# Opening of a fused attention and MLP kernel: warming matmuls, low parts, U and V loads, decoder pace

## The chip, the cores and the metric

The kernel runs on one core of one Trainium2 chip. The metric is device time in microseconds; a kernel's time is the median of its runs. The core's engines each follow their own row of instructions: TensorE (PE) multiplies matrices, VectorE (DVE), ScalarE (ACT) and GpSimd (POOL) work on tiles, and SyncE (SP) issues most transfers (DMAs).

## The reference

```python
# attention with random features, for q, k, v of shape (8, 8, 576, 64)
def phi(x):
    proj = np.einsum('bhsd,md->bhsm', x, omega)          # 128 features
    h = proj - np.sum(x * x, axis=-1, keepdims=True) / 2.0
    h = h - np.max(h, axis=-1, keepdims=True)
    return np.exp(h) / np.sqrt(m)
q_p, k_p = phi(q * scale), phi(k * scale)
kv = np.einsum('bhsm,bhsd->bhmd', k_p, v)
z = np.sum(k_p, axis=2)
num = np.einsum('bhsm,bhmd->bhsd', q_p, kv)
den = np.einsum('bhsm,bhm->bhs', q_p, z)[..., None] + 1e-06
x = (num / den), heads side by side                      # (8, 576, 512)
# then a low-rank mix over the sequence and an MLP
h = x.transpose(0, 2, 1) @ U @ V                         # rank 32
u = x + h.transpose(0, 2, 1)
out = u + np.maximum(u @ w_ch1, 0.0) @ w_ch2             # 512 -> 2048 -> 512
```

U, V and the two MLP weights come as 64-bit floats; everything else is 32-bit.

## The kernel before

Products are made in a reduced format of the same width (fp32r) from a high part and a low part of each operand: the high part is a cast, the low part the difference, and three matmuls (high by high, low by high, high by low) give one product.

**The attention.** The work is cut into 16 units: a pair of batches and a pair of heads. A unit's keys, and then its queries, are loaded as raw tiles of 64-column blocks and run through nine tiles of 128 rows. A *round* `r` has nine *steps* and handles two parts side by side: at first the keys of units 0 and 1, then in each round the keys of one unit and the queries of an earlier one. The second round (steps 9 to 17) takes keys 2 and queries 0, the third (steps 18 to 26) keys 3 and queries 1, and so on through 144 steps. The tile names are by place and not by content: `kt` is the first part's raw tile, `qt` the second's, so that `qt<-in_k_dram` is the keys of unit 1.

For three steps at a time a part is turned (`turn`, L614, a transpose on DVE into `xT`), cast (`high`, L618, on ACT into `xh`) and its low part is made (`low`, L622, on POOL into `xl`). `xT` has two buffers. A step then consists of `project` (L741 to L743, six matmuls into `p_p`, of which two buffers exist), `peak` (L749, the row maximum, on DVE into `nm`), `exp` (L756, four exponentials on ACT into `e`, three buffers), `use` (for keys a product with the values, L653 into `p_kv`; for queries two transposes, L679 into `p_q`, and a copy L684), and for queries `combine` (L692, L699, into `p_n`) and the normalizing of L709 to L724. A table `DELAY` sets how many steps after its own number each of these is written. The kernel is written step by step; a scheduler then orders the instructions of each engine, except that those wrapped in `K` (`keep_in_program_order`) stay in the order written among themselves.

**The loads.** All but a few loads of the attention are issued by SP, one after another, in the order written: omega, keys 0 and 1, their values, then in steps 0 and 1 of each round the keys and queries of the next round, and the values behind them.

**The decoder.** U, V and the weights are decoded from 64-bit to 32-bit floats beside the attention by a generator, `decoding`. A call of `advance(decoder)` moves it on by one piece of a job. Its first call issues the loads of U and of the first half of V (L329 to L332, L354); after six more calls the first job starts. A job is two ACT instructions (L132, L135), three on DVE (L150, L151, L154) and one on POOL (L174); then come the casts and low parts of the result (L336 to L339 for U, L360 to L363 for V, L246 to L255 for the first MLP weight). The step loop calls `advance` at `s % 3` not 0, two steps of three, for the first 54 steps, and at every second step after that; `left` limits the calls in all.

**The warming matmuls.** At the start, before any data has come, 12 matmuls of a zero tile `idle` are written, each into a tile `p_m` of its own, of which there is one buffer (L789). They are not kept in order.

**After the attention.** The low-rank mix of a pair of batches runs beside the next rounds (`mixing`: L401, L446, L414, L422), its result goes to DRAM; then the MLP's two products run as a seven-product scheme over blocks (L979, L1357), which takes the rest of the time.

Of the kernel before, what the change touches and what calls it, by code (L numbers as in the profile page):

```python
# [29 lines left out]
def performer_mlp_kernel(ctx: ExitStack, tc, q, k, v, omega, U, V, w1, w2, out):  # L30
# [74 lines left out]
    def depth():  # L105
        return 2 * RB if roomy else RB
# [8 lines left out]

    def decoding(jobs, late, lean, base, hold=(), defer=(), wide=0):

# [11 lines left out]
        def magnitude(i):  # L129
            if i < len(jobs):  # L130
                mags[i] = jobs[i][2]()
                K(nc.scalar.activation(out=mags[i], in_=f32(raws[i][:, :, 1]), func=AF.Abs))  # L132
                if i >= lean:
                    lows[i] = dec.tile([P, PIECE], I32, name="low", tag="de", bufs=2)[:, : jobs[i][1]]
                    K(nc.scalar.activation(out=lows[i], in_=raws[i][:, :, 0], func=AF.Copy, scale=2.0**-29))  # L135

        fetch(depth())
        for _ in range(late):
# [236 lines left out]
    EARLY = 1 + 2 + 4 * EARLY_GROUPS  # L375
    left = [6 + 5 * EARLY + 3]

# [221 lines left out]
    class Part:  # L599


        def __init__(self, src, i, place):
            self.src, self.unit = src, units[i]
            self.raw = io.tile([P, 2 * S], F32, name=("kt", "qt")[place])
            self.xh, self.xl = [], []
# [14 lines left out]
        def low(self):  # L620
            self.xl.append(wk.tile([P, G * P], F32R, name="xl", bufs=4))
            nc.gpsimd.tensor_tensor(out=self.xl[-1], in0=self.turned, in1=f32(self.xh[-1]), op=ALU.subtract)  # L622

# [149 lines left out]


    units = [(pair, hp) for pair in range(NP) for hp in range(NU)]
    keys = [Keys(i, i) for i in range(2)]
# [10 lines left out]
    nc.vector.memset(idle, 0.0)  # L787
    for _ in range(12):
        nc.tensor.matmul(ps.tile([P, P], F32, name="p_m", tag="p_m"), idle, idle, start=True, stop=True)  # L789
    om = mp.tile([P, 2, D], F32, name="om", tag="y", bufs=2)  # L790
# [16 lines left out]
    pom = ps.tile([P, P], F32, name="p_q", tag="p_q", bufs=2)  # L807
    nc.tensor.transpose(pom, om.rearrange("p j d -> p (j d)"), ident)
    for j in range(2):
        r = slice(j * D, (j + 1) * D)  # L810
        nc.scalar.copy(out=omh[r, j, :], in_=pom[r])
        nc.vector.tensor_tensor(out=oml[r, j, :], in0=pom[r], in1=f32(omh[r, j, :]), op=ALU.subtract)
# [16 lines left out]
    steps = {}  # L829
    decoder = decoding([u_job(), *v_jobs(), *weight_jobs()], 6, 0, -EARLY, defer=(EARLY + 3,), wide=EARLY)  # L830
    mixers = []
    x = None
    for s in range(NR * NT + 7):
# [34 lines left out]
        for st in at("turn0"):  # L868
            for p in st.group(0):
                p.turn()  # L870
        if s % (3 if s < 6 * NT else 2):
            advance(decoder)
# [40 lines left out]
        for st in at("project"):  # L913
            st.project()
        for st in at("use0"):
            st.use(0)
# [506 lines left out]
```

## Time and profile before

| | |
|---|---|
| three runs | 1064.04, 1067.19 and 1067.72 us; median 1067.19 |
| the profiled execution | 1067.31 us, of which 1065.2 us are the span from the first to the last instruction |
| mean granted clock of TensorE | 0.99 |
| busy share of PE, DVE, ACT, POOL | 97%, 81%, 58%, 48% of the span |
| first projection (step 0), second round (step 9) | at 8.33 us and 25.00 us |
| steps 54, 90 | at about 122.8 and 196.9 us |

The profile gives for each engine when an instruction started and how long it took. In a row of the timeline stand the start and the time in us, the engine, the line of the code, the operation, the tile written and the tiles read, and in square brackets how long the engine had been idle and what released it. In a row of windows stand the stretch, its length, the busy time and number of instructions of each engine shown, the granted clock of TensorE (1.00 is full), the share of the DMA engines and GB/s. In a row of groups stand the busy time in all, the mean of one in ns, and the idle time before them. A matmul of 32-bit operands that are not fp32r is recorded twice.

### The profile page before, as it was taken

Reading aid. Unit: us, or ns where it says so; the run is one execution under the profiler, and the core shown is the slowest. Engines: PE = TensorE matmul, PEld = TensorE weight load, DVE = VectorE, ACT = ScalarE, POOL = GpSimd, SP = SyncE. Lnnn points to the kernel's source line nnn. Section 1 sums busy time; section 2 is a strip of 40 time slices with the busy share of each in tenths; the row PEclk is TensorE's granted clock in tenths of the full one; section 3 lists DMA queues with packets and bytes.
Section 4 is the critical chain, followed back from the end, with each engine's and each line's share of the span. In section 5 each row is a group of like instructions: output and inputs, shape, how many; then the busy total and the mean of one; then the engine's idle time right before and its main releaser. Section 6 shows DMA issues by size and latency. Waiting matters only on the chain. (4 is left out here: it accounts for less than half of the span.)

```text
span 1065.2 us, 23872 instructions
## 1 busy us (share of the span) xinstructions
PE 1037.9 (97%) x8497; PEld 1014.9 (95%) x8497; DVE 864.0 (81%) x1510; ACT 615.5 (58%) x1479; POOL 506.3 (48%) x453
## 2 busy tenths in 40 slices
PE   8999999999998899999999999999999999999998
PEld 7898999989987899999999999999999999999998
DVE  4798898997998876766587576779999998989995
ACT  5889889889764646445445444754344444444442
POOL 3446957777334532341234214536645445445443
PEclk9899999999999899999999999999999999999999
DMA  9788787685337665976778857965455454454451
GB/s 133 137 159 149 146 191 136 126 206 106 89 61 192 170 174 141 234 223 173 176 201 198 212 156 222 302 201 184 142 169 169 139 173 165 141 171 164 142 173 43
DMA packets 380486, 175.51 MB, mean 165 GB/s; under 512 B 275664, under 2 KB 353488, under 8 KB 375760
## 3 DMA queue, kind: packets, MB, share of 16 engines
q1 hardware_dynamic: 378000, 173.70, 62.5%
q8 instruction: 67, 1.10, 0.4%
q10 hardware_dynamic: 2368, 0.30, 0.2%
q14 instruction: 51, 0.42, 0.1%
HBM read 109.97 MB, written 63.96 MB: 163 GB/s over the span
## 5 line engine op out<-in xcount | busy, mean ns | idle before, releaser
L756 ACT ACTIVATE e<-p_p,nm 128x128 f32<-128x128 f32 x576 | 166.1, 397 | 23.5 <-DVE nm L749 16.1
L1170 POOL TENSOR_TENSOR gs<-graw 128x512 f32<-128x512 f32 x70 | 105.6, 1513 | 145.4 <-DMA graw<-g 114.3
L1196 ACT CAST gh<-gs 128x512 fp32r<-128x512 f32 x140 | 86.9, 622 | 151.5 <-DVE gs L1170 76.9
L963 ACT ACTIVATE g<-g 128x512 f32<-128x512 f32 x105 | 66.5, 634 | 171.4 <-DVE g L967 100.3
L1203 DVE TENSOR_TENSOR gl<-gs,gh 128x512 fp32r<-128x512 f32 x140 | 133.8, 963 | 17.4 <-ACT gh L1196 15.8
L622 POOL TENSOR_TENSOR xl<-xT,xh 128x384 fp32r<-128x384 f32 x96 | 97.4, 1031 | 99.4 <-ACT xh L618 85.0
L749 DVE TENSOR_REDUCE nm<-p_p 128x4 f32<-128x512 f32 x144 | 98.2, 683 | 26.1 <-PE p_p L743 9.7
L174 POOL TENSOR_TENSOR wf<-wf,low 128x512 int32<-128x512 int32 (+2 forms) x35 | 45.1, 1288 | 145.6 <-ACT g L963 111.9
L741 PE MATMUL p_p<-omh,xh 128*128 128x256 f32 x288 | 93.3, 324 | 4.5 <-ACT e L756 3.0
L1282 POOL TENSOR_TENSOR u<-u,p 128x256 f32<-128x256 f32 x72 | 75.4, 1075 | 33.0 <-DVE u L1282 30.4
L1196 ACT CAST gh<-graw 128x512 fp32r<-128x512 f32 x107 | 64.3, 621 | 39.4 <-PE p_p L1357 9.5
L1203 DVE TENSOR_TENSOR gl<-graw,gh 128x512 fp32r<-128x512 f32 x107 | 80.8, 770 | 5.9 <-ACT gh L1196 4.8
L743 PE MATMUL p_p<-omh,xl 128*128 128x256 f32 x288 | 81.6, 284 | 0.6 <-POOL xl L622 0.6
L742 PE MATMUL p_p<-oml,xh 128*128 128x256 f32 x288 | 81.4, 283 | 0.0
L1357 PE MATMUL p_p<-wh,gh 128*128 128x256 f32 x288 | 81.1, 282 | 0.0
L1357 PE MATMUL p_p<-wh,gl 128*128 128x256 f32 x288 | 81.0, 281 | 0.0
L1357 PE MATMUL p_p<-wl,gh 128*128 128x256 f32 x288 | 80.9, 281 | 0.0
L1357 PE MATMUL p_q<-wh,gh 128*128 128x256 f32 x276 | 77.7, 282 | 0.0
L1357 PE MATMUL p_q<-wh,gl 128*128 128x256 f32 x276 | 77.6, 281 | 0.0
L1357 PE MATMUL p_q<-wl,gh 128*128 128x256 f32 x276 | 77.5, 281 | 0.0
L979 PE MATMUL p_n<-uh,wh 128*128 128x256 f32 x256 | 73.2, 286 | 3.9 <-DVE g L967 3.9
L699 PE MATMUL p_n<-kv,eT 128*128 128x65 f32 x512 | 72.3, 270 | 3.0 <-ACT eT L684 1.1
(267 smaller groups left out, 4023.2 us busy)
## 6 DMA issues: line engine op xcount, KB each, us to landing
graw<-g SPq DMA_DIRECT2D x36, 1024.0 KB, 5.2
g<-g SPq DMA_DIRECT2D x282, 128.0 KB, 2.3
raw<-in_moe_w_ch_dram SPq DMA_DIRECT2D x22, 512.0 KB, 4.6
u_dram<-ut SPq DMA_DIRECT2D x36, 256.0 KB, 2.4
u<-u_dram SPq DMA_DIRECT2D x36, 256.0 KB, 2.7
out_dram<-u SPq DMA_DIRECT2D x36, 256.0 KB, 2.3
kt<-in_k_dram SPq DMA_DIRECT2D x120, 72.0 KB, 3.0
qt<-in_q_dram SPq DMA_DIRECT2D x120, 72.0 KB, 2.7
```

What stands on the lines that cost most here:

```text
L622: nc.gpsimd.tensor_tensor(out=self.xl[-1], in0=self.turned, in1=f32(self.xh[-1]), op=ALU.subtract)
L741: nc.tensor.matmul(o, part.xh[g][:, ts], oh, start=True, stop=False)
L742: nc.tensor.matmul(o, part.xh[g][:, ts], ol, start=False, stop=False)
L743: nc.tensor.matmul(o, part.xl[g][:, ts], oh, start=False, stop=True)
L749: nc.vector.tensor_reduce(out=self.nm[:, :n], in_=self.pp[:, :n], axis=AX.X, op=ALU.max, negate=True)
L756: nc.scalar.activation(out=self.e[:, j, :], in_=self.pp[:, j, :], func=AF.Exp, bias=self.nm[:, j : j + 1])
L979: K(nc.tensor.matmul(p[:, f, :], x[:, k, fs], y[:, k, :], start=first, stop=(k == 1 and y is ul), skip_group_check=True,))
L1170: K(engine.tensor_tensor(out=to, in0=self.val[x], in1=self.val[y], op=op))
L1196: K(nc.scalar.copy(out=h, in_=v))
L1203: K(nc.vector.tensor_tensor(out=l, in0=v, in1=f32(h), op=ALU.subtract))
L1282: K(engine.tensor_tensor(out=out, in0=x, in1=y, op=ALU.add))
L1357: K(nc.tensor.matmul(acc[bank][:, half, :], x[:, ks], y[:, f, :], start=(now.s == 0 and k == 0 and half == 0 and x is h and y is wh), stop ...
```

## The change

- The 12 warming matmuls become 4 ahead of the transpose of omega, 12 behind it and 6 behind the projection of step 1. Those of one group share one tile, and all are kept in order.
- The low parts of the first two groups of three steps of keys 0 and keys 1 are made on DVE, not on POOL.
- The decoder waits for six more calls before it issues the loads of U and V (`rest=6`). They are then written behind the keys and queries of the third round.
- The step loop calls `advance` two times in three steps up to step 89, not 53; `left` is larger by six. By step 90 the decoder is where it was before.

```diff
-    def decoding(jobs, late, lean, base, hold=(), defer=(), wide=0):
+    def decoding(jobs, late, lean, base, hold=(), defer=(), wide=0, rest=0):
...
+        for _ in range(rest):
+            yield
         fetch(depth())
         for _ in range(late):
             yield
...
-    left = [6 + 5 * EARLY + 3]
+    left = [6 + 6 + 5 * EARLY + 3]
...
-            self.src, self.unit = src, units[i]
+            self.src, self.unit, self.i = src, units[i], i
...
-            nc.gpsimd.tensor_tensor(out=self.xl[-1], in0=self.turned, in1=f32(self.xh[-1]), op=ALU.subtract)
+            opening = isinstance(self, Keys) and self.i < 2 and len(self.xl) < 3
+            (nc.vector if opening else nc.gpsimd).tensor_tensor(
+                out=self.xl[-1], in0=self.turned, in1=f32(self.xh[-1]), op=ALU.subtract
+            )
...
+    BUSY = 12, 6
...
-    for _ in range(12):
-        nc.tensor.matmul(ps.tile([P, P], F32, name="p_m", tag="p_m"), idle, idle, start=True, stop=True)
+
+    def busy(n):
+        none = ps.tile([P, P], F32, name="p_m", tag="p_m")
+        for _ in range(n):
+            K(nc.tensor.matmul(none, idle, idle, start=True, stop=True))
+
+    busy(4)
...
     nc.tensor.transpose(pom, om.rearrange("p j d -> p (j d)"), ident)
+    busy(BUSY[0])
...
-    decoder = decoding([u_job(), *v_jobs(), *weight_jobs()], 6, 0, -EARLY, defer=(EARLY + 3,), wide=EARLY)
+    decoder = decoding([u_job(), *v_jobs(), *weight_jobs()], 6, 0, -EARLY, defer=(EARLY + 3,), wide=EARLY, rest=6)
...
-        if s % (3 if s < 6 * NT else 2):
+        if s % (3 if s < 10 * NT else 2):
             advance(decoder)
...
             st.project()
+            if st.s == 1 and s < NT:
+                busy(BUSY[1])
```

How the rows of the engines stand: on PE, before, the warming matmuls (`p_m`) lie around the transpose of omega and between the matmuls of steps 0 and 1.

```order
L789 MATMUL p_m<-idle 128x128 x2
L808 MATMUL p_q<-ident,om 128x128
L789 MATMUL p_m<-idle 128x128 x6
L741 MATMUL p_p<-omh,xh 128x256
L742 MATMUL p_p<-oml,xh 128x256
L741 MATMUL p_p<-omh,xh 128x256
L742 MATMUL p_p<-oml,xh 128x256
L789 MATMUL p_m<-idle 128x128
L743 MATMUL p_p<-omh,xl 128x256
```

On PE now, the same place:

```order
L798 MATMUL p_m<-idle 128x128 x4
L819 MATMUL p_q<-ident,om 128x128
L798 MATMUL p_m<-idle 128x128 x12
L746 MATMUL p_p<-omh,xh 128x256
L747 MATMUL p_p<-oml,xh 128x256
L746 MATMUL p_p<-omh,xh 128x256
L747 MATMUL p_p<-oml,xh 128x256
L748 MATMUL p_p<-omh,xl 128x256
```

Three more stood between and behind the following matmuls of steps 0 and 1 before; now none stands between them, and the last six stand behind step 1's last matmul.

On DVE, before, from the first transposes of the keys (`xT`) to the first row maxima (`nm`):

```order
L614 STREAM_TRANSPOSE xT<-kt 128x384
L614 STREAM_TRANSPOSE xT<-qt 128x384
L614 STREAM_TRANSPOSE xT<-kt 128x384
L614 STREAM_TRANSPOSE xT<-qt 128x384
L749 TENSOR_REDUCE nm<-p_p 128x4 x3
```

On DVE now, up to the third row maximum:

```order
L616 STREAM_TRANSPOSE xT<-kt 128x384
L616 STREAM_TRANSPOSE xT<-qt 128x384
L625 TENSOR_TENSOR xl<-xT,xh 128x384 x2
L616 STREAM_TRANSPOSE xT<-kt 128x384
L754 TENSOR_REDUCE nm<-p_p 128x4 x2
L625 TENSOR_TENSOR xl<-xT,xh 128x384
L616 STREAM_TRANSPOSE xT<-qt 128x384
L754 TENSOR_REDUCE nm<-p_p 128x4
```

The row maxima of steps 0 and 1 now stand ahead of the fourth transpose, and the low parts stand between; the fourth of them comes behind one more transpose.

On SP's queue, before, from the queries of the second round on (`x<-in_v_dram` are the values of keys 2, `kt` and `qt` behind them belong to the third round):

```order
L594 DMA qt<-in_q_dram 32x18x32 x8
L329 DMA raw<-in_moe_U_dram 128x4x64
L330 DMA raw<-in_moe_U_dram 64x64
L331 DMA raw<-in_moe_U_dram 64x64
L332 DMA raw<-in_moe_U_dram 128x4x64
L354 DMA raw<-in_moe_V_dram 32x576 x4
L636 DMA x<-in_v_dram 128x4x64 x2
L640 DMA x<-in_v_dram 64x2x64
L636 DMA x<-in_v_dram 128x4x64 x2
L640 DMA x<-in_v_dram 64x2x64
L594 DMA kt<-in_k_dram 32x18x32 x8
L594 DMA qt<-in_q_dram 32x18x32 x8
```

On SP's queue now, the same place:

```order
L596 DMA qt<-in_q_dram 32x18x32 x8
L641 DMA x<-in_v_dram 128x4x64 x2
L645 DMA x<-in_v_dram 64x2x64
L641 DMA x<-in_v_dram 128x4x64 x2
L645 DMA x<-in_v_dram 64x2x64
L596 DMA kt<-in_k_dram 32x18x32 x8
L596 DMA qt<-in_q_dram 32x18x32 x8
L331 DMA raw<-in_moe_U_dram 128x4x64
L332 DMA raw<-in_moe_U_dram 64x64
L333 DMA raw<-in_moe_U_dram 64x64
L334 DMA raw<-in_moe_U_dram 128x4x64
L356 DMA raw<-in_moe_V_dram 32x576 x4
```

U and V have moved behind the values of keys 2 and the third round's loads; the 42 issues in front of them are the same. Further on the scheduler also orders other instructions anew on all five engines, up to about step 90 (196.9 us); from there on the rows are the same as before.

## The prediction

> **What bounds the kernel now.** I read the page first, then PE's windows of 25 us, then the first 45 us by windows cut where the clock changes and by the timelines of PE, DVE, ACT and SP. PE's row on the page and two of its windows:
>
> ```profile
> PE 1037.9 (97%) x8497; PEld 1014.9 (95%) x8497; DVE 864.0 (81%) x1510; ACT 615.5 (58%) x1479; POOL 506.3 (48%) x453
> 25.00:50.00 25.00, 22.74 (x162) 21.57 (x162) 17.72 (x44) 19.10 (x63) 10.44 (x11) 0.86 0.71 138
> 425.00:450.00 25.00, 25.00 (x213) 25.00 (x212) 17.17 (x24) 11.37 (x21) 9.22 (x7) 1.00 0.93 239
> ```
>
> PE is the bound nearly everywhere: at 425 us it starts 213 matmuls in 25 us and never stops. At 25 to 50 us it starts 162, at a granted clock of 0.86. The whole change acts before about 200 us, since both programs' rows are alike on all five engines from there on; a lead won there is carried to the end, because what follows is PE work in the same order. So the question is how much PE loses at the start and how much of it the change removes. The stretch at 25 us, first by the clock (us, PE busy, matmuls, granted clock, DMA):
>
> ```profile
> 11.11:14.53 3.42, 2.19 (x15) 1.00 0.75 165
> 24.77:28.18 3.41, 1.53 (x10) 1.00 0.75 132
> 28.18:31.59 3.41, 3.41 (x18) 0.50 0.65 154
> 31.59:35.01 3.42, 3.42 (x18) 0.50 0.67 151
> 359.30:362.70 3.40, 1.56 (x13) 1.00 0.88 274
> 362.70:366.10 3.40, 3.40 (x19) 0.50 0.71 90
> ```
>
> From 28.18 to 35.01 us TensorE had half its clock: 6.83 us, a loss of about 3.4. Ahead of it lies a window of 3.41 us in which PE was busy for 1.53; 359.30 is another such window, and the clock halved behind it too. The window at 11.11, busy for 2.19, was followed by no drop. Why PE idled at 25 us, from PE's timeline:
>
> ```profile
> 25.32 0.28 PE L743 MATMUL p_p<-omh,xl 128*128 128x256 f32 x1
> 26.90 0.39 PE L741 MATMUL p_p<-omh,xh 128*128 128x256 f32 x1 [1.30 <-ACT xh L618]
> 27.98 0.44 PE L743 MATMUL p_p<-omh,xl 128*128 128x256 f32 x1 [0.58 <-POOL xl L622]
> ```
>
> and from those of DVE and of SP's queue:
>
> ```profile
> 25.73 0.58 DVE L614 STREAM_TRANSPOSE xT<-qt 128x384 f32<-128x384 f32 x1 [2.18 <-DMA qt<-in_q_dram]
> 15.89 4.38 SPq L594 DMA_DIRECT2D kt<-in_k_dram  x8
> 20.31 5.36 SPq L594 DMA_DIRECT2D qt<-in_q_dram  x8
> 25.71 0.50 SPq L329 DMA_DIRECT2D raw<-in_moe_U_dram  x1
> 28.12 1.89 SPq L354 DMA_DIRECT2D raw<-in_moe_V_dram  x4
> 38.73 5.31 SPq L594 DMA_DIRECT2D qt<-in_q_dram  x8
> ```
>
> Step 9, the first of the second round, needs the first queries. Their eight transfers leave SP at 20.31 to 25.67, right behind the keys', and DVE has waited 2.18 us for them when it starts at 25.73. ACT's cast follows, then the matmul at 26.90, then POOL's low part, then the matmul at 27.98. This gate at 26.90 to 28.2 us is set by SP's row of issues and not by anything PE does.
>
> **The change part by part.**
>
> *The faster start (warming matmuls, low parts on DVE).* What paced steps 0 to 3, by the timelines of DVE, ACT and PE:
>
> ```profile
> 11.21 0.58 DVE L614 STREAM_TRANSPOSE xT<-qt 128x384 f32<-128x384 f32 x1 [1.16 <-DMA qt<-in_k_dram]
> 11.82 1.29 DVE L749 TENSOR_REDUCE nm<-p_p 128x4 f32<-128x512 f32 x2
> 12.54 2.18 ACT L756 ACTIVATE e<-p_p,nm 128x128 f32<-128x128 f32 x8 [0.21 <-DVE nm L749]
> 13.74 0.39 PE L741 MATMUL p_p<-omh,xh 128*128 128x256 f32 x1 [1.18 <-ACT e L756]
> ```
>
> and what a low part costs, by the page's groups:
>
> ```profile
> L622 POOL TENSOR_TENSOR xl<-xT,xh 128x384 fp32r<-128x384 f32 x96 | 97.4, 1031 | 99.4 <-ACT xh L618 85.0
> L1203 DVE TENSOR_TENSOR gl<-graw,gh 128x512 fp32r<-128x512 f32 x107 | 80.8, 770 | 5.9 <-ACT gh L1196 4.8
> ```
>
> The first two reductions stood on DVE behind a transpose that waited for its DMA until 11.21; now they stand ahead of it, and the low parts are made on DVE. DVE has no 128x384 subtraction in the trace; POOL takes 1.03 us, and DVE's of 128x512 took 0.77, three quarters of which are 0.58. I take 0.6. The first exponentials can start at about 10.9 instead of 12.54. What is late next is the fourth low part: its transfer lands at 11.21 as before, and behind it come a transpose (0.58), a cast (0.51) queued behind eight exponentials, and a subtraction. So step 4 on gains 1.2 to 1.5 us, less than the 1.6 of the exponentials. And all of that ends at the gate: SP's first 42 issues are the same in both programs, none of them waits for this work, so step 9's second half still starts at 26.90. Worth 0; only PE's idle time ahead of the gate grows, from 1.3 us to about 2.8.
>
> *Ten more warming matmuls.* Each is two records:
>
> ```profile
> 1.09 1.65 PE L789 MATMUL p_m<-idle 128*128 128x128 f32 x4 [1.09 <-DVE idle L787]
> PEld p_m L789 <- PE p_m L789: 2.4, 7, 0.4
> ```
>
> Two took 1.65 us, 0.83 each, with a pause of some 0.35 to 0.4 for the one before, which one shared tile removes: about 0.45 each. Four end before the transposed omega needs PE (3.1 us), twelve run from 3.4 to about 8.8 while clock and data are awaited anyway; the first projection stood at 8.33. The six behind step 1 fill the wait that ended at 13.74. At most 0.5 us late, in front of the gate: 0.
>
> *The clock behind the gate.* With about 2.8 + 0.6 us of idle in front of it, nearly every position of a 3.41 us window takes in 1.9 us of idle or more, as 24.77 did, so the clock drops again, at a boundary somewhere between 25.4 and 28.8, for one window or two. Two windows would end between 32.2 and 35.6, one earlier. The loss behind 28 us is then half of what is left, 0.7 to 3.8 us against 3.4. From no drop at all (gain 3.4) to 0.4 more loss; I take a gain of 0.9.
>
> *U and V behind the third round's loads.* U's and V's eight issues take 25.71 to 30.06 (4.35 us); the values, keys and queries behind them move forward by that. Nobody waits for them: PE's waits from 28.2 to 122 us name no DMA:
>
> ```profile
> PE p_p L741 <- ACT e L756: 1.1, 6, 0.2
> ```
>
> (the longest of five, 3.5 us in all). Worth 0 by itself: it moves the next gate for a PE that ran ahead, but makes no lead. U and V themselves leave when the third round's queries have left, which is at 44.04 now and 4.35 sooner then, so between 39.7 and 44.0, and their first use moves by nine steps, some 18 us; no engine queues behind their late arrival.
>
> *The decoder out of the second round.* Decoding U and the first half of V took ACT's time there, by its timeline:
>
> ```profile
> 37.56 0.53 ACT L132 ACTIVATE wf<-raw 128x288 f32<-128x288 f32 x1
> 37.93 0.53 ACT L135 ACTIVATE low<-raw 128x288 int32<-128x288 uint32 x1
> 39.69 1.27 ACT L336 CAST su<-wf 128x320 fp32r<-128x320 f32 x3
> ```
>
> and this is what PE did beside it (windows: PE, PEld, DVE, ACT, POOL, clock, DMA):
>
> ```profile
> 38.00:40.00 2.00, 1.81 (x15) 1.47 (x13) 1.97 (x5) 2.00 (x8) 1.81 (x2) 1.00 0.81 130
> 40.00:42.00 2.00, 1.87 (x12) 1.45 (x12) 1.06 (x3) 2.00 (x8) 0.88 (x1) 1.00 0.87 142
> 46.00:48.00 2.00, 2.00 (x21) 2.00 (x19) 1.97 (x5) 1.29 (x5) 1.35 (x2) 1.00 0.69 171
> ```
>
> ACT is full from 38 to 42, and PE starts 27 matmuls where a full 4 us hold some 41: 14 at about 0.1 us, 1.4 us. The three rows of decoding are 2.3 us of ACT's time. The gain lies between 0 and 2.3; I take 1.3, near the matmuls missing.
>
> *The same work later.* U's casts now stand in the third round, whose ACT is less full: 0.5 lost, between 0 and 1.3. And six advances are regained in steps 54 to 89 (122 to 197 us), where 24 run instead of 18. ACT's decoding there, by its groups:
>
> ```profile
> L250 ACT CAST wh<-wf 128x256 fp32r<-128x256 f32 x9 | 4.1, 460 | 0.0
> L132 ACT ACTIVATE wf<-raw 128x512 f32<-128x512 f32 x3 | 2.1, 692 | 0.0
> L135 ACT ACTIVATE low<-raw 128x512 int32<-128x512 uint32 x3 | 2.0, 677 | 0.0
> L250 ACT CAST wh<-ws 128x256 fp32r<-128x256 f32 x4 | 1.8, 458 | 0.0
> ```
>
> and the windows of the last 27 of these steps, nine each:
>
> ```profile
> 140.40:159.40 19.00, 18.46 (x157) 17.66 (x155) 17.76 (x46) 16.61 (x55) 12.63 (x14) 1.00 0.88 202
> 159.40:177.40 18.00, 17.86 (x152) 17.12 (x151) 15.83 (x42) 17.25 (x56) 12.44 (x13) 1.00 0.83 158
> 177.40:196.90 19.50, 19.50 (x160) 18.72 (x159) 17.13 (x41) 18.75 (x62) 18.75 (x19) 1.00 0.63 120
> ```
>
> 9.9 us for 18 advances are 0.55 each, 3.3 us for six. It lies beside PE as long as ACT has idle time: 2.4 us in the first of these windows, 0.75 in each of the others, against 0.83 added (one and a half advances). Between 0 and 3.3; I take 0.5, since PE itself is all but full in these rows and ACT's idle time about covers the addition. The rows moved between 36 and 200 us beyond that can gain at most the waits listed, and may as well lose as much: 0, plus or minus 2.
>
> **The sum**, against the profiled execution's 1067.3 us (0.1 over the median shown): 0 - 0.9 - 1.3 + 0.5 + 0.5 = -1.2, so about 1066.0.
>
> **The rivals.** *The clock holds at the gate.* Then all 3.4 us come back, and with 1.3 and the 1.0 lost later the time is 1067.3 - 3.4 - 1.3 + 1.0, about 1063.5; 1061 if the later terms cost nothing and the moved rows gain. For it: the drop hangs on where a window falls, and the runs before spread from 1064.0 to 1067.7, 3.7 us, the price of one such stretch. Against it: PE's idle time there grows. The Trainium skill, TensorE: Matmul & The Clock Gate, section "HAM oscillation — how this bites in real kernels", has as its rule that only idle gaps of more than about 3.4 us re-throttle; by that rule neither the gaps of before nor those expected would cost the clock, and the sum would be this rival's. The trace disagrees: gaps of 1.30 and 0.58 us halved it.
>
> *All of it is absorbed.* The gate takes the start, the clock drops for two windows again, and U's casts cost in the third round what they cost in the second: 1067.3, give or take 1.
>
> *The denser decoder makes ACT the bound in steps 54 to 89.* Where PE has no slack now, each of six advances delays an exponential by its 0.55 us: 3.3 instead of 0.5, 1067.3 - 0.9 - 1.3 + 0.5 + 3.3 = 1068.9, slower. It decides when the added 0.83 us per nine steps exceed ACT's idle time, which in the last eighteen steps they just do; against it speak the 2.4 us idle in the nine before.
>
> **How the numbers follow.** My forecast has 0.46, the clock that holds 0.16, all absorbed 0.21, the denser decoder 0.13, and 0.04 is left for other ends. The likeliest one's own range is 1064 to 1068. The range reaches to 1061 for the first rival with gains in the moved rows, and to 1069.5 for the third. A measurement tells some 0.5% (5.3 us) from no change: faster means below 1061.9, which takes the first rival's better half (0.07) and 0.03 of the others; slower means above 1072.5, which no term here reaches alone (0.04).
>
> **What the profile after would show.** Right: DVE's transpose of the first queries still at about 25.7 us with a longer wait for its DMA (over 3 us); PE's step 9 second half at about 26.9; a stretch of half clock that begins between 25 and 29; no ACT decoding before 45 us and fuller PE windows between 36 and 48; ACT nearly full between 122 and 197. Wrong: PE's second round starting before 26 us, or no half clock between 25 and 36, or idle PE with releaser ACT between 122 and 197, or new waits of PE on DMA. The prediction fails most easily in the clock, whose windows fall anew in each run.

## The result, and the profile after

The changed kernel takes 1073.75 us (median of 12 runs, 1071.42 to 1075.88) against 1067.45 us (12 runs) for the kernel before: ratio 1.0062, 95% interval 1.0043 to 1.0082. It is slower by 6.3 us, where 1066.0 was forecast. The profiled execution took 1073.76 us, its span is 1071.7, 6.5 longer than before.

PE's row on the page of the changed kernel, and then its windows of the start (us, PE, PEld, DVE, ACT, POOL, clock, DMA):

```profile
PE 1041.0 (97%) x8517; PEld 1016.9 (95%) x8517; DVE 869.2 (81%) x1514; ACT 613.9 (57%) x1479; POOL 500.8 (47%) x449
```

```profile
21.69:25.11 3.42, 1.87 (x17) 1.73 (x17) 1.66 (x4) 2.68 (x9) 0.99 (x1) 1.00 0.88 141
25.11:28.52 3.41, 3.29 (x15) 2.99 (x15) 1.52 (x3) 1.95 (x6) 1.22 (x2) 0.50 0.82 155
31.93:35.35 3.42, 3.42 (x18) 3.42 (x18) 1.50 (x3) 1.31 (x6) 0.00 (x0) 0.50 0.85 137
38.00:40.00 2.00, 2.00 (x21) 2.00 (x20) 1.19 (x4) 1.36 (x7) 1.37 (x2) 1.00 0.70 110
40.00:42.00 2.00, 2.00 (x21) 2.00 (x21) 1.79 (x5) 1.85 (x8) 0.00 (x0) 1.00 0.39 85
```

The first two lines of windows show where the start's lead ends: PE, ahead by its faster start, idles earlier than before, the window from 21.69 is busy for 1.87 us, and the clock is halved from 25.11 to 35.35, three windows where it had been two. From 38 to 42 us PE now starts 42 matmuls where it had started 27: the decoder is gone from there.

What PE waits for at 23.83 is not yet the queries, by the rows of DVE and PE:

```profile
21.39 0.58 DVE L616 STREAM_TRANSPOSE xT<-kt 128x384 f32<-128x384 f32 x1 [2.37 <-DMA kt<-in_k_dram]
21.89 1.25 DVE L754 TENSOR_REDUCE nm<-p_p 128x4 f32<-128x512 f32 x2
...
23.83 0.39 PE L746 MATMUL p_p<-omh,xh 128*128 128x256 f32 x1 [1.55 <-ACT e L761]
```

The transpose of keys 2 stands in DVE's row ahead of two row maxima and waits 2.37 us for its transfer. The maxima behind it start at 21.89, ACT's exponentials at 22.64, and PE idles for 1.55 us until they are done with one of the two buffers of `p_p`. In the kernel before the same transpose, at 20.26, did not wait. PE's matmul at 23.83 is the first of step 8, which had started at 23.41: the start's lead, 1.3 us at step 6, is gone before the place that the prediction calls the gate.

The first queries' transpose and the second half of step 9, from the timelines of DVE and PE:

```profile
25.95 0.58 DVE L616 STREAM_TRANSPOSE xT<-qt 128x384 f32<-128x384 f32 x1 [0.36 <-DMA qt<-in_q_dram]
...
26.88 0.58 PE L746 MATMUL p_p<-omh,xh 128*128 128x256 f32 x1
```

Both stand about where they stood before (25.73, 26.90). The whole loss arises later. Against before the changed kernel stood, by the start of each step's first matmul, at -1.9 us at step 3, -1.3 at step 6, +0.8 at step 9, -1.5 at step 18, -2.0 at step 36, -0.3 at step 54, +2.3 at step 63, +5.3 at step 72, +6.7 at step 81, +6.5 at step 90, and at +6.4 to +6.5 from there on. Steps 54 to 89 in one row of windows, first the kernel before:

```profile
122.80:196.90 74.10, 73.40 (x609) 70.13 (x608) 67.76 (x169) 68.14 (x222) 54.94 (x57) 1.00 0.77 158
```

and the changed kernel:

```profile
122.50:203.40 80.90, 77.31 (x607) 71.95 (x607) 73.57 (x171) 70.58 (x229) 61.81 (x65) 0.98 0.72 151
```

PE has the same matmuls (a record or two is missing), but the stretch is 6.8 us longer: 1.7 of it are a window at half clock that was not there before, 5.1 are time at full clock. DVE is busy 5.8 us more, POOL 6.9, ACT 2.4. A large single loss stands at 158 us, by its windows:

```profile
158.22:161.64 3.42, 1.40 (x10) 0.93 (x9) 3.37 (x10) 2.68 (x11) 3.42 (x5) 1.00 0.88 142
161.64:165.05 3.41, 3.41 (x18) 3.41 (x18) 2.21 (x5) 0.81 (x4) 2.65 (x4) 0.50 0.97 197
```

and by rows of PE, DVE, ACT and POOL from its timelines:

```profile
159.15 0.58 PE L684 MATMUL p_q<-ident,e 128*128 128x128 f32 x2 [0.67 <-ACT e L761]
161.07 0.63 PE L704 MATMUL p_n<-kv,eT 128*128 128x65 f32 x4 [1.34 <-DVE rec L715]
...
157.06 1.24 DVE L153 TENSOR_SCALAR wf<-wf 128x512 uint32<-128x512 uint32 x1
158.22 0.15 DVE L714 TENSOR_SCALAR rec<-p_n 128x4 f32<-128x4 f32 x1
158.88 1.50 DVE L156 SCALAR_TENSOR_TENSOR wf<-raw,wf 128x512 uint32<-128x512 uint32 x1
160.30 0.17 DVE L715 RECIPROCAL rec<-rec 128x4 f32<-128x4 f32 x1
...
157.82 0.43 ACT L252 CAST wh<-ws 128x256 fp32r<-128x256 f32 x1
158.12 0.43 ACT L252 CAST wh<-wf 128x256 fp32r<-128x256 f32 x1
158.69 2.21 ACT L761 ACTIVATE e<-p_p,nm 128x128 f32<-128x128 f32 x8
...
157.00 1.01 POOL L625 TENSOR_TENSOR xl<-xT,xh 128x384 fp32r<-128x384 f32 x1 [2.93 <-ACT xh L620]
158.84 1.00 POOL L625 TENSOR_TENSOR xl<-xT,xh 128x384 fp32r<-128x384 f32 x1
159.79 1.18 POOL L257 TENSOR_TENSOR wl<-wf,wh 128x256 fp32r<-128x256 f32 x1
```

ACT makes two more casts of the weight (L252), a cast and a copy of the attention's own, and only then, at 158.69, starts the exponentials, the first of whose row maxima was done at 157.1. DVE spends 1.24 and 1.50 us on two decoding instructions, and two reciprocals (L715) come behind them, at 160.30 and 160.84; PE's matmul at 161.07 waits for a reciprocal, by its row. PE idles 2 us in all, the window from 158.22 is busy for 1.40 us, and the next one runs at half clock. (By the Trainium skill, TensorE: Matmul & The Clock Gate, section "HAM oscillation — how this bites in real kernels", whose rule names idle gaps of more than about 3.4 us, gaps of 0.67 and 1.34 us would not have cost the clock; here they did, as did the one of 1.55 us at 23.83.) The two DVE instructions start 0.06 and 0.04 us after a POOL instruction; the same shift took 0.42 us at 140.50, with POOL idle.

### The profile page after: what moved, and what is told of

Its sections match the earlier page's. It is cut to its first block, busy times and chain, and to the rows that moved or that the text cites. A ratio compares the mean times of both kernels' runs of the same rounds, so it can differ in the third digit from the quotient of the medians.

```text
span 1071.7 us, 23911 instructions
## 1 busy us (share of the span) xinstructions
PE 1041.0 (97%) x8517; PEld 1016.9 (95%) x8517; DVE 869.2 (81%) x1514; ACT 613.9 (57%) x1479; POOL 500.8 (47%) x449
## 5 line engine op out<-in xcount | busy, mean ns | idle before, releaser
L1217 DVE TENSOR_TENSOR gl<-gs,gh 128x512 fp32r<-128x512 f32 x140 | 136.1, 979 | 17.5 <-ACT gh L1210 15.6
L625 POOL TENSOR_TENSOR xl<-xT,xh 128x384 fp32r<-128x384 f32 x92 | 94.7, 1044 | 114.0 <-ACT xh L620 99.1
```

What stands on the lines that cost most here:

```text
L625: (nc.vector if opening else nc.gpsimd).tensor_tensor(out=self.xl[-1], in0=self.turned, in1=f32(self.xh[-1]), op=ALU.subtract)
L1217: K(nc.vector.tensor_tensor(out=l, in0=v, in1=f32(h), op=ALU.subtract))
```

## The experiments

A kernel's time hangs partly on where half-clock windows fall, so I give beside the median the length of steps 54 to 89 less half of the half-clock time in it ("full clock", one profile each), and the mean over a kernel's runs of span times granted clock. Ratios are to the kernel before on the same chip, where its median lay between 1064.7 and 1067.9 us, so the medians of two rows compare less well than their ratios. Kernels below "left out" leave out part of the decoding (and g1 one column in 512).

| kernel | median us | ratio, 95% interval | steps 54-89, full clock | span x clock |
|---|---|---|---|---|
| before | 1067.45 | | 74.1 | 1055.0 to 1056.8 in five sets |
| changed | 1073.75 | 1.0062 (1.0043-1.0082) | 79.2 | 1061.7 |
| e1 old pace | 1073.53 | 1.0063 (1.0036-1.0091) | 76.5 | 1059.5 |
| e2 pace alone | 1072.60 | 1.0048 (1.0016-1.0079) | 78.3 | 1060.6 |
| e3 start alone | 1065.83 | 1.0011 (0.9982-1.0041) | 73.0 | 1056.5 |
| e4 decoder alone | 1071.06 | 1.0044 (1.0019-1.0068) | 79.1 | 1061.1 |
| j1 phase 1 | 1069.32 | 1.0026 (1.0005-1.0048) | 79.3 | 1061.3 |
| j2 phase 2 | 1073.87 | 1.0071 (1.0049-1.0093) | 78.0 | 1060.6 |
| g1 odd shapes | 1073.36 | 1.0058 (1.0030-1.0086) | 79.2 | 1061.4 |
| h1 accumulator | 1072.94 | 1.0072 (1.0044-1.0100) | 80.5 | 1057.8 |
| h2 start, accumulator | 1065.26 | 1.0000 (0.9985-1.0016) | 75.4 | 1053.8 |
| h3 start, clamp on POOL | 1084.07 | 1.0182 (1.0153-1.0211) | 77.2 | 1063.8 |
| i1 start, halves | 1068.19 | 1.0001 (0.9976-1.0026) | 74.1 | 1057.9 |
| i2 before, halves | 1070.52 | 1.0034 (1.0011-1.0057) | 73.3 | 1058.1 |
| **left out:** f1 changed, no DVE | 1060.88 | 0.9932 (0.9903-0.9961) | 77.0 | 1053.1 |
| f2 before, no DVE | 1063.49 | 0.9960 (0.9934-0.9985) | 75.2 | 1051.7 |
| f3 changed, less ACT | 1065.63 | 0.9996 (0.9976-1.0017) | 77.1 | 1053.9 |
| f4 changed, short POOL | 1073.63 | 1.0064 (1.0036-1.0092) | 80.0 | 1062.7 |
| i3 changed, lean | 1062.12 | 0.9945 (0.9925-0.9964) | 76.9 | 1051.5 |
| i4 before, lean | 1056.39 | 0.9891 (0.9863-0.9920) | 72.7 | 1048.2 |

### Which edit costs: e1 to e4

*e1*, the changed kernel with the old pace:

```diff
-        if s % (3 if s < 10 * NT else 2):
+        if s % (3 if s < 6 * NT else 2):
```

> The changed kernel with the old pace (two advances in three steps only up to step 53, then every second); the decoder's late start and the six added calls stay, so the decoder ends about twelve steps later. Theory D, the denser decoder of steps 54 to 89 costs the loss: steps 54 to 90 fall back to about 74 us and the time to 1066 to 1067.5 us, no more than at par with the kernel before. Rival S, the loss is due to the start or to U and V's later place, which reach steps 54 to 90 through the scheduler's new order: the time stays at 1072 to 1074.

*e2*, the kernel before with the new pace alone:

```diff
-        if s % (3 if s < 6 * NT else 2):
+        if s % (3 if s < 10 * NT else 2):
```

> The kernel before with only the pace changed (two advances in three steps up to step 89; start, U, V and the number of calls as before). Theory D: steps 54 to 90 take 78 to 81 us instead of 74, and the time is 1071 to 1074, slower by about 0.5%. Rival S: within 1 us of the kernel before, 1066.5 to 1068.5.

*e3*, the changed kernel with e1's edit and

```diff
-    left = [6 + 6 + 5 * EARLY + 3]
+    left = [6 + 5 * EARLY + 3]
...
-    decoder = decoding([...], 6, 0, -EARLY, defer=(EARLY + 3,), wide=EARLY, rest=6)
+    decoder = decoding([...], 6, 0, -EARLY, defer=(EARLY + 3,), wide=EARLY)
```

> The kernel before with only the warming matmuls and the low parts on DVE changed; U, V and the decoder as before. Theory D with the prediction's first term (the start is absorbed by the wait for the second round's queries): 1066 to 1068, no difference. If the longer stretch of half clock behind the wait costs what it is worth (10.2 us instead of 6.8), 1068 to 1069. Rival S, start part: 1072 to 1074.

*e4*, the kernel before with e2's edit, e3's two the other way round, and the lines of `rest` in `decoding`:

```diff
+        for _ in range(rest):
+            yield
         fetch(depth())
```

> The kernel before with only the decoder's edits (U and V behind the third round's loads, six more calls, the denser pace up to step 89); the start as before. Theory D: 1071 to 1074, like the changed kernel, with 78 to 81 us in steps 54 to 90. Rival S, start part: 1066 to 1067.

Steps 54 to 89 of e1:

```profile
123.70:200.20 76.50, 73.95 (x609) 69.73 (x607) 70.71 (x168) 67.54 (x220) 53.62 (x56) 1.00 0.76 157
```

of e2:

```profile
126.30:206.40 80.10, 76.98 (x608) 71.76 (x607) 70.84 (x168) 70.54 (x224) 60.61 (x63) 0.98 0.72 150
```

of e3:

```profile
125.80:201.50 75.70, 75.04 (x608) 72.42 (x608) 67.02 (x167) 67.77 (x221) 53.96 (x56) 0.96 0.72 149
```

and of e4:

```profile
123.80:204.60 80.80, 77.23 (x607) 71.88 (x607) 73.49 (x170) 70.51 (x229) 61.76 (x65) 0.98 0.73 153
```

Theory D holds in e2, e3 and e4: the start alone makes no difference, and the pace alone costs about what the change costs, in these steps, without U and V being moved at all. It misses in e1: steps 54 to 89 were to come back to about 74 us and are at 76.5, and the time, 1073.53, is the one that Rival S had. In e1's profile steps 54 to 107 take 112.9 us, 113.2 in the kernel before, so the old pace is at par there. But the decoder now runs on to about step 122, and steps 108 to 125, 36.9 us in the kernel before, take 40.3. e2 shows the other side: its decoder is six calls ahead at step 90, and steps 90 to 107 take 36.8 us instead of 39.1, so 2.3 of the 4.2 us lost come back. So it isn't the pace as such: six calls cost 3.4 us in steps 108 to 125 and 4 to 5 us in steps 54 to 89, and 2.3 us come back where they are missing. In the kernel before they stood in the second round, beside a PE that waited or had half its clock. Taking them out had gained 0.3 us by step 54 in the changed kernel, and e1 and e4 stood 0.9 and 1.0 us behind there. No run moves U and V without the six calls, so what their place alone costs is open.

### DVE or ACT: f1, f2 and f3

*f1* and *f2* drop the DVE part of the weights' decoding:

```diff
-                if slot:
+                if slot and i < 3:
                     tc.keep_in_program_order(slot())
```

> The changed kernel without the three DVE instructions of each weight's decoding (U and V keep theirs; the weights are then wrong in value, ACT's and POOL's part of the decoding stay). Theory P (each moved decoder call costs because its DVE instructions wait for POOL to be done, so that the row maxima behind them on DVE are late): steps 54 to 90 take 72 to 75 us at full clock and the time is 1060 to 1066 us. Rival A (the added casts and activations on ACT cost): steps 54 to 90 stay at 78 us or more and the time at 1071 to 1074.

> The kernel before with the same DVE instructions left out. Theory P: it gains less than the changed kernel does by the same edit, since fewer of these instructions lie in its crowded steps: 1061 to 1066, so that the two kernels without them are within 2 us of each other. Rival A: 1066 to 1067.5, and the distance of 5 to 6 us to the changed kernel stays.

Without these instructions the changed kernel is no slower than the other any more: 1060.88 against 1063.49, 2.6 us apart where theory P had up to 2. The attention (up to step 143) takes 308.7 and 308.4 us in their profiles, where it was 313.5 and 307.1. So in this pair the loss is gone with DVE's part. DVE isn't all of it: steps 54 to 89 fell only to 77.0 us, not to 75 or less, and f1 has a stall of its own at 163 us, with ACT alone. ACT's rows ahead of it:

```profile
161.36 0.44 ACT L252 CAST wh<-wf 128x256 fp32r<-128x256 f32 x1
161.67 0.70 ACT L132 ACTIVATE wf<-raw 128x512 f32<-128x512 f32 x1
162.25 0.67 ACT L135 ACTIVATE low<-raw 128x512 int32<-128x512 uint32 x1
162.79 1.93 ACT L761 ACTIVATE e<-p_p,nm 128x128 f32<-128x128 f32 x7
```

A cast and the two decoding instructions of the next piece hold up the exponentials, whose maximum stood at 161.9.

*f3* drops one ACT instruction of each piece:

```diff
-                K(nc.scalar.activation(out=mags[i], in_=f32(raws[i][:, :, 1]), func=AF.Abs))
+                if i < 3:
+                    K(nc.scalar.activation(out=mags[i], in_=f32(raws[i][:, :, 1]), func=AF.Abs))
...
-                lambda: nc.vector.tensor_scalar(m, m, _LEAST, _MOST, ALU.max, ALU.min),
+                lambda: nc.vector.tensor_scalar(m, m if i < 3 else f32(high), _LEAST, _MOST, ALU.max, ALU.min),
```

> The changed kernel without one of the two ACT instructions of each weight's decoding (the absolute value; DVE's clamp reads the raw word itself, so the weights' signs are treated wrongly). It takes 0.69 us of ACT for each piece. Rival A (ACT is what the moved decoder calls cost): steps 54 to 90 take 75 to 77 us at full clock and the time is 1068 to 1070. Theory P: 78 us or more, time 1071 to 1074 (less 0 to 3 us for the same instruction in the second phase, whose steps behind 307 us tell).

77.1 us at full clock and 1065.63: a little outside Rival A's 75 to 77 in these steps, and below both Rival A's 1068 and theory P's 1071. Part of it comes from the second phase: from step 143 on f3 takes 754.7 us, the changed kernel 758.2. So lightening DVE takes 2.2 us off these steps, lightening ACT 2.1, in one profile each; neither theory was right alone. Both sizes are uncertain: f2, the same edit as f1 in the kernel before, made these steps 1.1 us longer, so another order of rows moves them by as much as half of this.

### What makes DVE's instructions long: f4, g1, h1, h2 and h3

*f4* cuts POOL's part of the weights' decoding:

```diff
+                    cut = n if i < 3 else n // 8
-                    nc.gpsimd.tensor_tensor(out=m.bitcast(I32), in0=m.bitcast(I32), in1=e, op=ALU.add)
+                    nc.gpsimd.tensor_tensor(out=m.bitcast(I32)[:, :cut], in0=m.bitcast(I32)[:, :cut], in1=e[:, :cut], op=ALU.add)
...
+            c = 32 if self.g < EARLY_GROUPS else 2 * P
-            K(engine.tensor_tensor(out=l, in0=self.v[LEFT[i]], in1=f32(h), op=ALU.subtract))
+            K(engine.tensor_tensor(out=l[:, :c], in0=self.v[LEFT[i]][:, :c], in1=f32(h)[:, :c], op=ALU.subtract))
```

> The changed kernel with POOL's part of the weights' decoding cut to an eighth (64 of 512 columns of the final addition, 32 of 256 columns of each low part of the first two weight groups; the rest of the low parts is set to zero by POOL between steps 118 and 131). DVE's and ACT's instructions stay. Theory P: DVE's tensor_scalar instructions of the decoder fall from means of 0.72 and 0.96 us to below 0.7, steps 54 to 90 take 74 to 77 us at full clock and the time is 1066 to 1070. Rival A: no change on ACT, steps 54 to 90 at 78 us or more, time 1071 to 1074.

Theory P misses, and the numbers are Rival A's (80.0 us, 1073.63): the means of the two tensor_scalar instructions were 0.93 and 0.90 us, not below 0.7. POOL's time fell by 12 us, but what DVE's instructions meet is mostly the `xl` low parts of 1.0 us each (L625), which stayed. So this run does not tell DVE's wait for POOL from work on ACT.

*g1* changes the shapes of the two tensor_scalar instructions:

```diff
-                lambda: nc.vector.tensor_scalar(m, m, _LEAST, _MOST, ALU.max, ALU.min),
+                lambda: nc.vector.tensor_scalar(*odd(m), _LEAST, _MOST, ALU.max, ALU.min),
...
+            def odd(t):   # the shift likewise: *odd(words(m))
+                if n < PIECE:
+                    return t, t
+                return [t[:, :511].rearrange("p (a b) -> p a b", a=a) for a in (7, 73)]
```

> The changed kernel with the decoder's two tensor_scalar instructions on DVE written over 511 of 512 columns as 7 x 73 out and 73 x 7 in (one column of 512 stays undecoded). By the Trainium skill, VectorE: DVE Perf Modes, section Mode 2x_2P, such odd and unequal shapes get no second port. Theory P with that rule: each of them takes some 0.55 to 0.7 us whatever POOL does, where they took 0.42 with POOL idle and up to 1.25 with POOL busy; steps 54 to 90 take 75 to 78 us at full clock, the time is 1067 to 1071. Rival A, or if the shape changes nothing: means of 0.72 and 0.96 us with a wide spread as now, time 1072 to 1074.

Their durations are those of the changed kernel to 40 ns (0.41 to 1.06, 0.42 to 1.27). Each side is one unbroken run of 511 words, so the shapes may well be merged to equal ones before they reach the engine; the rule isn't tested by it.

*h1* and *h2* add an accumulator to the clamp (L152), in the changed kernel and in e3:

```diff
-                lambda: nc.vector.tensor_scalar(m, m, _LEAST, _MOST, ALU.max, ALU.min),
+                lambda: nc.vector.tensor_scalar(m, m, _LEAST, _MOST, ALU.max, ALU.min,
+                    accum_out=dec.tile([P, 1], F32, name="acc", bufs=2)),
```

> The changed kernel in which the first of the decoder's DVE instructions (the clamp, a tensor_scalar) also writes its accumulator. The Trainium skill, SBUF - State Buffer, section Who interferes with whom, leaves that form out of those that take the second port shared with GpSimd. Theory P (DVE's two-port instructions wait for POOL): the clamp takes a steady 0.6 to 0.7 us, its spread below 0.2 us, whatever POOL does (it took 0.41 to 1.03 in steps 54 to 89), while the shift behind it, unchanged, still goes from 0.42 to 1.25. The time goes to 1070 to 1073. Rival W (the durations are due to something else, as memory traffic): the clamp still goes beyond 1 us where POOL works, time 1073 to 1075.

> The kernel with the start's edits alone, and the same clamp with an accumulator. In the profile of the start alone one clamp took 5.06 us while POOL worked without a break from 117.6 to 122.7 us. Theory P: no clamp beyond 0.8 us, the time 1063 to 1066, up to 2 us below the start alone. Rival W: clamps of over 1 us remain, 1065 to 1068.

DVE's clamps (with accumulator) and shifts (unchanged) of h1, from its timeline:

```profile
136.72 0.67 DVE L152 TENSOR_SCALAR_CACHE_REDUCE wf<-wf 128x512 f32<-128x512 f32 x1
139.04 0.42 DVE L153 TENSOR_SCALAR wf<-wf 128x512 uint32<-128x512 uint32 x1
150.72 0.67 DVE L152 TENSOR_SCALAR_CACHE_REDUCE wf<-wf 128x512 f32<-128x512 f32 x1
184.20 0.67 DVE L152 TENSOR_SCALAR_CACHE_REDUCE wf<-wf 128x512 f32<-128x512 f32 x1
188.70 3.95 DVE L153 TENSOR_SCALAR wf<-wf 128x512 uint32<-128x512 uint32 x1
```

The clamp takes 0.67 us each time, though a POOL instruction runs beside each, and no clamp of h2 takes more than 0.69; the shift, which has no accumulator, goes from 0.42 to 3.95. So the clamp's long times were a wait for POOL, as theory P has it, and Rival W is out. It agrees with the Trainium skill, SBUF — State Buffer, section "Who interferes with whom": a DVE instruction in a two-port mode and GpSimd exclude each other for whole instructions, and the form that writes out its accumulator has no such mode. The time, though, stayed: 1072.94, and h2 is at par with the kernel before. A wait less in one instruction of three does not show, and h1 has one shift of 3.95 us and two half-clock windows of its own in these steps.

*h3*, in e3:

```diff
-                lambda: nc.vector.tensor_scalar(m, m, _LEAST, _MOST, ALU.max, ALU.min),
+                lambda: (nc.gpsimd if i >= 3 else nc.vector).tensor_scalar(m, m, _LEAST, _MOST, ALU.max, ALU.min),
```

> The kernel with the start's edits alone, and the clamps of the weights made on POOL in place of DVE (about 1.0 to 1.3 us each there). Theory P: DVE loses one waiting instruction in three, POOL has room (54.9 of 74 us busy in steps 54 to 89): 1062 to 1066. If POOL's longer row makes the other two wait longer, or its low parts late: 1067 to 1070.

Slower by 1.8%, beyond both expectations. Half of it is in the second phase, which decodes too (768.5 us from step 143 on, 10.4 more than before). More work on POOL lengthens the row that DVE's other instructions wait for: the remaining decoding instructions of steps 54 to 89 took 11.8 us on DVE (8 of them), against 8.0 for 11 in the kernel before.

### Order or crowding: i3, i4, j1 and j2

*i3* and *i4*: f3's edit, and of the DVE slots only the clamp, in the changed kernel and in the kernel before:

```diff
-                if slot:
+                if slot and (i < 3 or j == 0):
```

> The changed kernel with one DVE and one ACT instruction in the decoding of each piece of a weight in place of three and two (absolute value, shift and merge are left out, so the weights are wrong; POOL's work, casts and low parts stay). Theory P+A (the loss in steps 54 to 89 is crowding, DVE's waits for POOL and ACT's work together in one chain): steps 54 to 90 at 73 to 75.5 us of full clock, and the attention as long as that of the kernel before with the same left out, within 1.5 us. Rival O (the loss is an unlucky order of the scheduler's, whatever the load): 76.5 us or more, the attention 3 us or more longer.

> The kernel before with the same left out, to be compared with it. Theory P+A: the attention within 1.5 us of the changed kernel so cut, both within 2 us of the kernel before in steps 54 to 90 (74 us). Rival O: the distance of 5 to 6 us between the two kernels stays.

The distance of 5.7 us stayed, as Rival O had it. But i3 has one stall of a kind that no other kernel's steps 54 to 89 had at that size, by DVE's and PE's timelines:

```profile
147.19 0.69 DVE L425 TENSOR_TENSOR ut<-ph,x 128x512 f32<-128x512 f32 x1 [3.16 <-DMA u_dram<-ut]
148.94 1.11 PE L705 MATMUL p_n<-kv,eT 128*128 128x65 f32 x4 [3.05 <-DVE eT L690]
```

DVE waits for the store of an earlier `ut`, and PE behind it; the clock then halves for two windows. Without its 3.1 us steps 54 to 89 would be at 73.8, 1.1 above i4. That is a subtraction and no proof, so the same density was run in two other orders. *j1* and (with 2 for 1) *j2*, in the changed kernel:

```diff
-        if s % (3 if s < 10 * NT else 2):
+        if (s + (1 if 6 * NT <= s < 10 * NT else 0)) % (3 if s < 10 * NT else 2):
```

> The changed kernel with the two calls in three of steps 54 to 89 placed one step off: the same number of decoder calls there, in another order of rows on all engines. Theory C (crowding: so many calls cost there in any order): steps 54 to 90 take 77.5 to 81 us of full clock and the time is 1070 to 1075. Rival O (the order of before was a good one and that of the changed kernel a bad one by chance): full-clock times in steps 54 to 90 of the two phases spread from 74 to 81 us, at least one of them below 76, and its time is 1065 to 1069.

> The same with the calls two steps off. Theory C: 77.5 to 81 us of full clock in steps 54 to 90, time 1070 to 1075, within 2 us of the other phase. Rival O: the two phases differ by over 3 us in these steps.

Steps 54 to 89 of j1:

```profile
122.50:201.80 79.30, 75.57 (x605) 70.08 (x604) 69.05 (x172) 70.42 (x228) 61.56 (x66) 1.00 0.74 157
```

and of j2:

```profile
123.50:201.50 78.00, 75.56 (x607) 70.14 (x607) 70.69 (x171) 70.94 (x228) 61.24 (x66) 1.00 0.75 155
```

No half clock in either, and 79.3 and 78.0 us: theory C's numbers for these steps. Its times came only in part: j1's 1069.32 is below the 1070 expected, and the two phases are 4.6 us apart by their medians, where up to 2 was expected. The denser pace has now been seen in five orders (e2, h1, j1, j2, and the changed kernel, e4 and g1, which are alike here), at 78.0 to 80.5 us, the old pace at 73.0 to 76.5 in six kernels (before, e1, e3, h2, i1, i2; h3, with its clamps on POOL, is apart). j1's profile has 18.2 us at half clock, j2's 22.5 and the changed kernel's 24.9, and by span times clock j1 stands with the others. So the denser decoder costs 3.9 to 6.4 us at full clock, against 74.1, in every order tried; against the mean of the old pace's six, 74.4, the mean of the five, 79.1, is 4.7 us more. One profile each stands behind these, and the closest two (78.0 and e1's 76.5) are 1.5 us apart. Where half-clock windows fall adds to that or takes from it. j1's DVE spent 9.4 us on 14 decoding instructions there, the changed kernel's 13.5, with the same full-clock time: how much of the price is DVE's wait for POOL and how much its and ACT's plain work stays open.

### The gate at the second round: i1 and i2

*i1* and *i2*: SP's issues of the second round, in e3 and in the kernel before:

```diff
                 new[0].load(0)
-                new[0].load(1)
+                if r:
+                    new[0].load(1)
...
                 new[1].load(0)
+                if not r:
+                    new[0].load(1)
                 new[1].load(1)
```

> The start's edits alone, and SP's issues of the second round in another order: first half of keys 2, first half of queries 0, second halves, where all eight of keys 2 stood ahead. The first queries' transfers then leave about 2.2 us (four issues) earlier. Theory G (the start's lead ends at the wait for the first queries, as the prediction's first term has it): DVE's first transpose of queries stands at about 23.5 instead of 25.7 us, the second round comes 1.5 to 2.5 us earlier, and the time is 1062 to 1065, 1 to 3 us below the kernel before. Rival N (the lead of the start ends elsewhere too, or the clock takes it): 1065 to 1068.

> The kernel before with the same order of issues alone. Theory G: the wait at 26.90 us falls away, since PE comes to it at about 25; gain about 1 us and, where the clock's stretch of 6.8 us at half speed goes with it, up to 3.4 more: 1062.5 to 1066.5. Rival N: 1066 to 1068.

DVE's first transpose of queries and PE's next wait, i1:

```profile
23.47 0.58 DVE L616 STREAM_TRANSPOSE xT<-qt 128x384 f32<-128x384 f32 x1 [0.31 <-DMA qt<-in_q_dram]
33.92 0.41 PE L658 MATMUL p_kv<-x,e 128*128 128x65 f32 x2 [1.25 <-DMA x<-in_v_dram]
```

The transpose stands at 23.47, as expected, and no clock drop follows; i1 leads by 4.8 us at step 12 (3.4 of them are the half clock that the kernel before had), by 1.9 at step 18 and by 0.4 to 0.5 from step 36 on. It is Rival N's outcome, at 0.2 us beyond its range: behind the gate stands a wait for the values, 1.25 us, and what takes the rest is not shown. i2, at 1070.52 and slower by 0.3%, is beyond both of its expectations; its profile has the long clamp of the last section, and how often its other runs have it is not on record. No version here that decodes everything is faster than the kernel before.

## Why the prediction was wrong

- **The faster start, worth 0: right in its result, not in the place.** e3 measures no difference, and step 9's second half started at 26.88, as forecast. But PE already waits at 23.83, behind the transpose of keys 2 with the row maxima behind it on DVE, which the prediction doesn't have. So PE's idle time there did not grow from 1.3 to about 2.8 us; it was 1.55. The sign named for it, a wait of over 3 us ahead of the queries' transpose, did not show: a row maximum at 24.90 stands between, and 0.36 us were left.
- **The clock behind the gate, -0.9: wrong in size.** It was forecast for one or two windows from 25.4 to 28.8 and lasted three from 25.11, which costs 1.7 us more than before, where 0.9 less was taken. It differs from profile to profile: of the 13 with the new start and the old order of issues, five have half clock between 25 and 36 us (three windows in the changed kernel, e3, f3 and h1, two in h3), and eight have none there. So the argument that nearly every position of a window brings a drop doesn't hold: e1's PE had gaps of 1.22, 0.82 and 0.34 us there, and kept its clock until 45.23.
- **The decoder out of the second round, -1.3, and U's casts in the third, +0.5: right up to step 36.** PE's windows from 38 to 42 filled, ACT's first decoding stands at 44.10 (the sign had none before 45), and the lead at step 36 was 2.0 us. It was gone by step 54 (-0.3): steps 36 to 44 take 20.3 us instead of 18.5, and 19.9 to 21.3 at full clock in e1, e4, j1 and j2, which have the same late U and V. Where parts of the weights' decoding are left out with U and V as late (f1, f3, i3), they take 18.5 to 19.0, so there too the decoder's work as a whole, and not U's casts alone, seems to be the price.
- **The same work later, +0.5: the step that failed.** It measured +5.1 at full clock and +1.7 of half clock behind the stall at 158 us. Two things were wrong. The price of an advance was ACT's 0.55 us alone; DVE's part (11 instructions, 8.0 us for the 18 advances of before, 0.44 each) was left out of it, and POOL's. And ACT's idle time was taken as cover, 2.4 and 0.75 us per nine steps. That time is no free place: 3.3 us of ACT's idle time between 122 and 197 us ended with a row maximum for its next exponential, and at 158 us, and in f1 at 162 us, decoding instructions on ACT put off the next exponentials and PE waited. Six advances at 0.55 are 3.3 us, with DVE's 0.44 6.0: the 3.9 to 6.4 us measured lie about there, as if almost nothing covered them. That is a comparison of sizes and no test; which engine's part costs how much stays open (j1). The third rival had the place and the mechanism of a lost cover, but with ACT alone as its engine; its 3.3 us are about half of the 6.8 measured.
- **"Idle PE with releaser ACT between 122 and 197"** was named as a sign against the forecast, and stands at 159.15.
- **The moved rows, 0 plus or minus 2,** cover part of what orders do: i3's one stall is 3.1 us, and old-pace kernels spread over 3.5 us in steps 54 to 89.

## What to carry to other kernels

When PE is all but full and the two engines that feed it in a chain, here DVE and ACT, are each over 90% busy, an idle share is not cover: price moved work at the sum over all engines in the chain, and expect most of it on the path. Work that stands beside a bound engine's wait or beside its half clock can be nearly free there: taking the decoder out of the second round had gained at most 0.6 us by step 54 in the kernels that decode everything. Look for that before moving it. And a row that waits for another engine's port is found by its spread: the same instruction at 0.42 and at 1.24 us.

## What the runs showed of the hardware

One DVE instruction of 0.42 us can wait for POOL through several POOL instructions, not only for the one that runs. DVE, POOL and PE around 118 us in e3's profile:

```profile
117.94 5.06 DVE L152 TENSOR_SCALAR wf<-wf 128x512 f32<-128x512 f32 x1
...
117.60 1.28 POOL L403 TENSOR_TENSOR ml<-x,mh 128x512 fp32r<-128x512 f32 x1
118.84 0.73 POOL L257 TENSOR_TENSOR wl<-wf,wh 128x256 fp32r<-128x256 f32 x1
119.53 1.96 POOL L625 TENSOR_TENSOR xl<-xT,xh 128x384 fp32r<-128x384 f32 x2
121.45 1.26 POOL L403 TENSOR_TENSOR ml<-x,mh 128x512 fp32r<-128x512 f32 x1
...
124.74 0.48 PE L684 MATMUL p_q<-ident,e 128*128 128x128 f32 x1 [3.08 <-ACT e L761]
```

POOL worked without a gap from 117.60 to 122.71, and DVE's clamp, begun at 117.94, ended at 123.00; the row maxima and exponentials behind it came late, PE idled 3.08 us and lost two windows of clock. In h1 a shift begun at 188.70 ended at 192.65, 0.28 us behind a row of POOL's. Whether it comes to this is a matter of timing. Beside the same instructions on POOL the same clamp took 5.05 us in e2 (at 118.17) and 4.70 in i2 (120.09), but 1.26 in the kernel before (118.68) and 1.20 in i1 (118.24). e2, e3 and i2 take 24.3 to 24.5 us for steps 45 to 53, the kernel before and i1 20.5. So kernels with the old and with the new start can meet it, and it is part of why one order of the same work differs from another.
